# An inverse transform stage on 64-row instead of 128-row matmul tiles, with a new instruction order

## The chip, the cores and the metric

The kernel runs on one core of a Trainium2 chip. The metric is the device time of one launch in microseconds (us). A core has a matmul engine (TensorE, PE in the profile; its weight loads are listed apart as PEld), a vector engine (VectorE, DVE), a scalar engine (ScalarE, ACT), GpSimd (POOL) and a queue engine that issues most transfers (SyncE, SP). Each engine works through its own list of instructions in order and waits for the others by semaphores.

## What is computed

Two layers, each a long causal convolution with gates (A) and a feed-forward block (B), on 2048 positions of 512 channels. Both layers use the same k, v and filters, so the convolution result `y` is the same in both and the kernel computes it once.

```python
def _A_ref(q, k, v, shift_k, ssm_k, ssm_D):
    for t in range(ks):                      # ks = 4 taps
        k_shift = k_shift + k_pad[:, t:t + S, :] * shift_k[:, ks - 1 - t][None, None, :]
    kv = k_shift * v
    kv_f = rfft(kv padded to 2S, axis 1); kf_f = rfft(ssm_k padded to 2S)
    y = irfft(kv_f * kf_f)[:, :S, :]  (bfloat16)
    y = y + kv * ssm_D[None, None, :]
    return q * y

def _B_ref(x, w1, b1, w2, b2):
    y = _layernorm(x, axis=-1)
    h = _gelu(jnp.einsum("bsd,df->bsf", y, w1) + b1)
    return jnp.einsum("bsf,fd->bsd", h, w2) + b2

x = A_q
x = x + _A_ref(_layernorm(x, axis=-1), A_k, A_v, A_shift_k, A_ssm_k, A_ssm_D)
x = x + _B_ref(_layernorm(x, axis=-1), B_w1, B_b1, B_w2, B_b2)
# and the same two lines once more
```

## The kernel before

**Staging.** The 2048 positions are treated as two halves of 1024. For each half, the filter and the gated input go through a transform in two matmul stages. `stage1` makes eight tiles (names h1_0, h1_1 for the filter of the first and the second half, x1_0, x1_1 for the input). `stage2` makes eight more (h2_0, h2_1, x2_0, x2_1). The filter's spectrum is copied to a partner buffer by a DMA exchange (`swap`, eight transfers of 256 KB). VectorE multiplies the spectra (line 475, tag x2_0 for the first half). The inverse has two stages: `inverse1` (i1_0, i1_1; lines 677 to 704) and `inverse2` (i2_0, i2_1; line 706 on). Around that stand the transposes of the raw filter (`turn`, tags ht0 and ht1, line 561), the four-tap filter (fir0 to fir7), and thirteen blocks of the two layers: normalize and gate (q, y), normalize again (z), first feed-forward matmuls with gelu (m1, lines 920 and 925), second matmuls and add (m2, lines 954 and 958). Blocks 0 to 8 belong to the first half and fill the engines while the second half's transform runs.

**inverse1.** Each of its eight tiles (j = 0 to 7) takes eight channel groups, and for each group two products p and q, [128 x 128] each, against a 128-row table `R_U`. In i1_0 (`split` False) that is 16 matmuls a tile: a 128x128 weight load and 128 moving columns each. In i1_1 (`split` True) the upper and the lower 64 rows are separate matmuls: 32 matmuls a tile, each with a 64x128 weight load and 64 moving columns, which leaves out the half of the table that is zero for those rows; the two row halves write to two different PSUM banks. The output of a tile is the same [128 x 1024] in both; it is brought to SBUF by one instruction on ScalarE or VectorE (line 480 or 481, called an eviction here). `inverse2` multiplies over all eight tiles of i1, so it begins after the last of their evictions. Tiles j = 0 to 3 need the first 64-channel-group products (g = 0) of all eight x2_0 tiles, j = 4 to 7 the second (g = 1).

**Order.** Nothing is scheduled at run time. The program is a list of 1187 numbered operations. `SEQ` gives the order in which they are put on the engines' queues, `ENGS` names the engine (p, a, v for GpSimd, ScalarE, VectorE) of each operation that has a choice, and `BANKS` the first PSUM bank of each PSUM tile. All three are tables that were found by a search and written out. A tile of these stages takes two banks of 2 KB per partition, so there are four places (banks 0, 2, 4, 6); a matmul tile waits until the eviction of the tile that had its place before is done. `sync` derives all semaphore waits from data and banks.

**Numbers used below.** As each engine's list is in order, an operation's instruction is found by counting along its engine's part of `SEQ`:

| operations | what |
|---|---|
| 75/76, 77/78, ... 89/90 | h2_0 tiles 0 to 7: matmuls / eviction |
| 133/134, 129/130 | x1_0 tiles: matmuls / eviction |
| 139/140, 141/142, 145/146 | last three ht1 tiles: 8 transposes / eviction |
| 147/148, ... 161/162 | h1_1 tiles 0 to 7: matmuls / eviction |
| 163/164, 167/168, ... 191/192 | x2_0 tiles 0 to 7: matmuls / eviction; the two numbers after a pair are its products on VectorE (line 475) |
| 218/219, ... 232/233 | i1_0 tiles j = 0 to 7: matmuls (line 695) / eviction |
| 234 to 243 | i2_0, five tiles (line 717), matmuls / eviction |
| 244 to 267 | h2_1: matmuls and two combinations each (line 788) |
| 284 to 287 | four loads of v for the second half (SP) |
| 268 to 275 | the second half's exchange (SP) |
| 396 | first gate product of block 0 (y0), needs the first i2_0 tile |
| 404 | first transposes of block 0 (line 908) |

In the profile's order, ScalarE's nineteen evictions from 30.37 us on are 176, 164, 88, 188, 168, 150, 180, 192, 184, 160, 162, 142, 158, 156, 221, 225, 223, 231, 233; the next three are 227, 152, 235.

Of the kernel before, what the change touches and what calls it, by code (L numbers as in the profile page):

```python
# [36 lines left out]
class Prog:  # L37
# [361 lines left out]
def bass_interleave_layers__ssm_conv_h3__mixer_channel_mlp__prompt_kernel(  # L399
# [38 lines left out]
    R_1, R_2, R_3, R_8, R_4, R_5, R_6 = [place(n) for n in (8192, 8192, 8192, 11776, 8192, 8192, 8192)]  # L438
# [334 lines left out]
    P.op(POOL, lambda e: e.tensor_copy(SG, sg), 190.0, reads=[sg], writes=[SG])  # L773

    P.tag = "i1_0"
    inverse1(R_1, R_2, R_3, False)
    P.tag = "i2_0"
    inverse2(R_3, R_YT[0])

# [215 lines left out]
```

## Time and profile before

| | us |
|---|---|
| median of 3 runs (lowest, highest) | 236.24 (235.94, 237.43) |
| the profiled execution, whole | 235.91 |
| its span, first to last instruction | 234.0 |
| PE busy | 222.7 |
| DVE busy | 178.7 |
| ACT busy | 164.5 |
| POOL busy | 55.5 |

The granted TensorE clock is 1.00 throughout. The difference between 235.91 and 234.0 (1.9 us) lies around the span. Times in the views are us from the span's start. In a row of the order of time, the first number is the start, the second the duration, `x` the count of merged instructions, and in brackets stands the idle time before it and what ended it. A busy matmul row includes the pipeline's latency, so a single 128-column matmul shows 219 ns while eight tiles of sixteen take 7.38 us together.

### The profile page before, as it was taken

To read this page: it belongs to the slowest core of one execution; us is meant where nothing else is said; L and a number is where in the kernel's file an instruction comes from. 1 tells how busy PE (TensorE), PEld (TensorE's weight loads), DVE (VectorE), ACT (ScalarE), POOL (GpSimd) and SP (SyncE) were. 2 spreads that over 40 slices of the span, in tenths; PEclk is the share of its full clock that TensorE was granted. 3 is DMA by queue.
4 is the path that set the end of the run, shared out by engine and by line. 5 is a ranking of instruction groups with operands and counts; after the bars stand their busy time and mean duration, and the time that the engine had idled before them with its cause. 6 is when DMAs were issued, how large, how long until landed. Compare 5 with 4: busy or idle time off the path is not lost.

```text
span 234.0 us, 6498 instructions
## 1 busy us (share of the span) xinstructions
PE 222.7 (95%) x2743; PEld 147.1 (63%) x2765; DVE 178.7 (76%) x362; ACT 164.5 (70%) x262; POOL 55.5 (24%) x113
## 2 busy tenths in 40 slices
PE   7989887999999999999999999999999999999995
PEld 3878776967868596677966576644444444444454
DVE  0699998999999999999999988781777569410222
ACT  2789999989968688999879986488058216802710
POOL 2270132006403405639303331204011120200000
PEclk9999999999999999999999999999999999999999
DMA  6999489928994360033500313401300130170202
GB/s 185 381 386 305 147 229 274 324 65 150 144 211 126 70 158 3 1 48 72 155 4 3 90 24 68 134 3 22 69 0 3 28 62 0 23 115 0 90 0 92
DMA packets 40106, 24.93 MB, mean 107 GB/s; under 512 B 23591, under 2 KB 33677, under 8 KB 40077
## 3 DMA queue, kind: packets, MB, share of 16 engines
q1 hardware_dynamic: 39778, 24.36, 39.7%
q8 instruction: 22, 0.36, 0.7%
q10 hardware_dynamic: 298, 0.16, 0.4%
q14 instruction: 8, 0.06, 0.1%
HBM read 13.23 MB, written 2.10 MB: 66 GB/s over the span
## 4 chain that ended last, share of the span: by engine, by line
PE 58%; DVE 24%; ACT 10%; issue 2%; POOL 2%; DMA 2%; SPq 0%; DVEq 0%
PE ps L920 23%; PE ps L954 23%; DVE ar L475 13%; ACT ar L480 9%; PE ps L695 4%; DVE sm L831 3%; PE ps L590 2%; DMA ar<-in_A_ssm_k_dram 2%; DVE ar L672 2%; DVE ar L958 2%; DVE ar L641 2%; PE ps L717 1%; POOL sm L836 1%; PE ps L578 1%; PE ps L635 1%
## 5 line engine op out<-in xcount | busy, mean ns | idle before, releaser
L925 ACT ACTIVATE ar<-ps,sm 128x256 bf16<-128x256 f32 (+5 forms) x143 | 65.7, 523 | 33.2 <-PE ps L920 32.9
L920 PE MATMUL ps<-ar 128*128 128x256 bf16 (+5 forms) x569 | 81.9, 297 | 0.4 <-ACT ar L480 0.2
L480 ACT ACTIVATE ar<-ps 128x1024 bf16<-128x1024 f32 (+3 forms) x77 | 71.1, 998 | 11.0 <-PE ps L578 3.4
L954 PE MATMUL ps<-ar 128*128 128x512 bf16 (+1 forms) x323 | 75.9, 379 | 1.5 <-issue 0.6
L920 PEld LDWEIGHTS ps<-ar 128*128 128x128 bf16 (+1 forms) x572 | 52.9, 100 | 27.5 <-ACT ar L480 1.1
L475 DVE TENSOR_TENSOR ar<-ar 128x512 bf16<-128x512 bf16 (+2 forms) x104 | 62.7, 646 | 1.5 <-ACT ar L480 0.8
L954 PEld LDWEIGHTS ps<-ar 128*128 128x128 bf16 (+1 forms) x341 | 32.4, 98 | 35.3 <-ACT ar L925 0.4
L958 DVE TENSOR_TENSOR ar<-ar,ps 128x512 bf16<-128x512 bf16 x31 | 20.8, 680 | 32.9 <-PE ps L954 32.9
L831 DVE BATCH_NORM_STATS2 sm<-ar 128x6 f32<-128x512 bf16 x64 | 42.5, 685 | 0.5
L856 ACT ACTIVATE ar<-ar,sm 128x512 bf16<-128x512 bf16 x39 | 30.6, 813 | 12.9 <-DVE sm L843 8.8
L836 POOL TENSOR_SCALAR sm<-sm 128x2 f32<-128x2 f32 (+2 forms) x22 | 9.9, 449 | 89.0 <-DVE sm L832 88.8
L838 POOL TENSOR_TENSOR sm<-sm 128x2 f32<-128x2 f32 (+2 forms) x26 | 21.7, 834 | 25.1 <-DVE sm L836 23.1
L590 PE MATMUL ps<-ar 128*128 128x64 bf16 x512 | 18.4, 193 | 1.5 <-DVE ar L481 0.7
L578 PE MATMUL ps<-ar 128*64 128x128 bf16 x512 | 17.9, 221 | 1.8 <-ACT ar L480 1.2
L590 PEld LDWEIGHTS ps<-ar 128*128 128x128 bf16 x512 | 16.8, 98 | 3.6 <-DVE ar L481 1.3
L578 PEld LDWEIGHTS ps<-ar 128*64 128x64 bf16 x512 | 14.9, 110 | 4.8 <-ACT ar L480 1.9
L481 DVE CAST ar<-ps 128x1024 bf16<-128x1024 f32 x12 | 14.6, 1218 | 1.2 <-PE ps L578 0.9
L846 POOL TENSOR_SCALAR sm<-sm 128x1 f32<-128x1 f32 x34 | 15.1, 460 | 1.6
L695 PE MATMUL ps<-ar 64*128 64x64 bf16 (+1 forms) x384 | 12.4, 203 | 1.0 <-DVE ar L475 0.9
L695 PEld LDWEIGHTS ps<-ar 64*128 64x128 bf16 (+1 forms) x384 | 11.8, 113 | 2.2 <-DVE ar L475 1.0
L857 DVE TENSOR_SCALAR ar<-ar,sm 128x512 bf16<-128x512 bf16 x25 | 10.3, 415 | 2.7 <-POOL sm L846 2.5
L788 DVE SCALAR_TENSOR_TENSOR ar<-ar,sm,ps 128x512 bf16<-128x512 bf16 x16 | 11.1, 740 | 0.3 <-PE ps L590 0.3
(45 smaller groups left out, 93.5 us busy)
## 6 DMA issues: line engine op xcount, KB each, us to landing
ar<-ar SPq DMA_DIRECT2D x16, 256.0 KB, 4.0
ar<-tab_s SPq DMA_DIRECT2D x9, 256.0 KB, 6.3
ar<-in_A_ssm_k_dram SPq DMA_DIRECT2D x8, 256.0 KB, 5.9
ar<-in_A_q_dram SPq DMA_DIRECT2D x8, 256.0 KB, 4.4
ar<-in_A_v_dram SPq DMA_DIRECT2D x8, 256.0 KB, 5.0
out_dram<-ar SPq DMA_DIRECT2D x7, 256.0 KB, 2.5
ar<-in_B_w_dram SPq DMA_DIRECT2D x4, 344.0 KB, 5.2
ar<-in_B_w_dram SPq DMA_DIRECT2D x5, 256.0 KB, 5.2
```

Source lines behind the costliest of these rows:

```text
L475: return P.op(eng, lambda e: e.tensor_tensor(o, a, b, op), dur, reads=[a, b] + list(more), writes=[o])
L480: return e.activation(dst, src(), AF.Copy)
L578: r = e.matmul(Q(tl, 64 * ri, 64, i * 128, [1, 128]), w, m, start=True, stop=True)
L590: r = e.matmul(Q(tl, 0, 128, i // 8 * 512 + i % 8 * 4, [32, 16], [1, 4]), w, m, start=True, stop=True)
L695: r = e.matmul(Q(tl, 0, 128, i, *([32, 16], [1, 4]) if split else ([1, 128],)), w, m, start=n == 0, stop=n == 1)
L831: P.op(DVE, lambda e, sj=sj, x=x: e.bn_stats(sj, x), 600.0, reads=[x], writes=[sj])
L838: P.op(POOL, lambda e: e.tensor_tensor(r, v, hf, ALU.pow), 420.0 + 149.0 * n, reads=[v, hf], writes=[r])
L856: return e.activation(o, x, AF.Identity, bias=u, scale=r)
L920: r = e.matmul(Q(tl, 0, rows, 0, [1, w]), a, m, start=dk == 0, stop=dk == 3)
L925: P.op(ACT, lambda e, dst=dst, tl=tl, rows=rows, bias=bias, w=w: e.activation(dst, Q(tl, 0, rows, 0, [1, w]), AF.Gelu_apprx_tanh, bias=bia ...
L954: r = e.matmul(Q(tl, 0, 128, 0, [1, 512]), ins[fc][0], ins[fc][1], start=fc == 0, stop=fc == 10)
L958: P.op(DVE, lambda e, x=x, tl=tl: e.tensor_tensor(x, x, Q(tl, 0, 128, 0, [1, 512]), ALU.add), 604.0, reads=[x], writes=[x], tile=tl)
```

## The change

The first half's call takes the form of the second half's, and the three tables are replaced. The number of operations stays 1187, the lengths of the tables as well. No new function is called.

```diff
@@ (from line 773 on)
     P.tag = "i1_0"
-    inverse1(R_1, R_2, R_3, False)
+    inverse1(R_1, R_2, R_3, True)
     P.tag = "i2_0"
     inverse2(R_3, R_YT[0])
```

```diff
     SEQ = (
...
-        84, 145, 88, 187, 165, 171, 188, 96, 177, 167, 95, 172, 168, 149, 97, 296, 150, 146, 179, 98, 183, 170, 180,
-        195, 191, 173, 210, 157, 192, 208, 174, 202, 169, 184, 201, 159, 189, 196, 161, 303, 160, 207, 181, 155, 211,
-        185, 162, 203, 141, 193, 206, 142, 194, 224, 166, 158, 220, 190, 156, 186, 218, 178, 436, 221, 222, 182, 225,
+        84, 145, 88, 187, 188, 165, 96, 171, 177, 167, 95, 168, 149, 172, 97, 150, 98, 296, 179, 146, 195, 170, 180,
+        191, 210, 173, 196, 159, 192, 208, 174, 183, 201, 169, 184, 157, 207, 161, 189, 303, 211, 160, 155, 193, 203,
+        202, 181, 162, 185, 194, 141, 166, 142, 224, 190, 158, 220, 186, 178, 156, 218, 182, 436, 221, 582, 222, 219,
...
     ENGS = (
-            "pvavvvvvavpvpapapaaavaaaaavaavaavavvvppvvvaavvaaavaavvaaaaaaaaavvaaaaavaaaavaaaaaaapppvaaaaaaaaaaaaaaaaaa"
+            "pvavvvvvavpvpapapaaavaaaaaaaavaavavvvvpvvvaavvaaavaavvaaaaaaaaavvaaaavaaaavaaaaaaavpppaaaaaaaaaaaaaaaaaa"
...
     BANKS = (
-            "26624320240260660466027405640260464422140204626240406006442460424046462022442640460444626002206020640220"
+            "26624320240260660466027405640260464422140204626024406006442462424046462002442240460640446202220006040402"
...
```

The entries of the tables in and just before the changed stage that differ:

| operation | before | after |
|---|---|---|
| 78 (eviction, h2_0 tile 1) | VectorE | ScalarE, between 122 and 134 |
| 176 (eviction, x2_0 tile 3) | ScalarE | VectorE, between 90 and 584 |
| h1_1 tile of 157/158 | bank 2 | bank 0 |
| h1_1 tile of 159/160 | bank 4 | bank 2 |
| h1_1 tile of 161/162 | bank 0 | bank 4 |
| i1_0 tile of 218/219 | bank 2 | bank 0 |
| i1_0 tile of 224/225 | bank 0 | bank 2 |
| order of h1_1 matmuls | 157, 159, 161, 155 | 159, 157, 161, 155 |

The ht1 tile of 141/142 stays on bank 4; the tile that has bank 4 just before it is 159/160 before and 161/162 after. ScalarE's order from 88 to 235 is the same in both (88, 188, 168, 150, 180, 192, 184, 160, 162, 142, 158, 156, 221, 225, 223, 231, 233, 227, 152, 235), and so is TensorE's order of the i1_0 tiles (224, 220, 218, 222, 230, 232, 228, 226).

Later in the order: one i2_1 eviction goes from ScalarE to VectorE; of the small statistics operations up to the last product sum of the second half (tag sum), four go from GpSimd to VectorE and one back; the number of TensorE operations ahead of the first i1_1 tile is 204 in both. On SP, the v loads 286 and 287 stood ahead of all exchange transfers of the second half, and now stand behind the first (268) and the second (271) of them. Normalizations of the q and z steps change engine in both directions (ten from ScalarE to VectorE, twelve the other way).

More of the change, by code (lines that the diff above doesn't have):

```diff
@@ L45 @@
         0, 46, 8, 45, 35, 2, 6, 3, 5, 36, 12, 9, 1, 10, 11, 25, 4, 44, 217, 7, 56, 197, 15, 50, 16, 57, 14, 13, 47,
[3 rows of a table removed]
[3 rows of a table added]
         111, 68, 394, 117, 33, 112, 395, 119, 29, 123, 118, 124, 143, 32, 144, 131, 120, 81, 113, 474, 213, 79, 82,
[50 rows of a table removed]
[50 rows of a table added]
     ENGS = (
-            "pvavvvvvavpvpapapaaavaaaaavaavaavavvvppvvvaavvaaavaavvaaaaaaaaavaaaaavaaaavaaaaaaapppvaaaaaaaaaaaaaaaaaa"
-            "avaaaaaaaaapvapvvavpvppaappvvpvaavpaappaappaappaappaappavppvappaappaappvappaapvaapvavvavvvvvapvvvvvppvaa"
-            "avvvvaappavvapvavavpvvava")
+            "pvavvvvvavpvpapapaaavaaaaaaaavaavavvvvpvvvaavvaaavaavvaaaaaaaaavvaaaavaaaavaaaaaaavpppaaaaaaaaaaaaaaaaaa"
+            "avaaaaaaavapvapvvavpvvpaappvvppaavpaappaappaappaapvaappavppvavvaappaappvappaappaavpvaavvvvaaappaavvppaav"
+            "vvvvavvvpaavavvvavvvvavav")
     BANKS = (
-            "26624320240260660466027405640260464422140204626240406006442460424046462022442640460444626002206020640220"
-            "04023022660051677767117660640311026376367637332542537030213654742352762454741476061377362300423726574027"
-            "07315704314621527766215047034261015330227471565340011503350731745320154030276054756")
+            "26624320240260660466027405640260464422140204626024406006440462424046462002442240460640446202220006040402"
+            "20201200661071175760610706761354673263266337232241657763022741351603667540723566150777263632670156541304"
+            "32172437425406650215234545702175254221347040501613506136707146104347507513610560112")
     def __init__(self, nc):
```

100 rows, old and new, of the table SEQ are left out of this document.

## The prediction

> **What bounds the kernel now.** I read the page's head first, then busy time by stretch, then the chain that ended last, then the order of time around the changed stage.
>
> ```profile
> span 234.0 us, 6498 instructions
> PE 222.7 (95%) x2743; PEld 147.1 (63%) x2765; DVE 178.7 (76%) x362; ACT 164.5 (70%) x262; POOL 55.5 (24%) x113
> ```
>
> ```profile
> 41.00:56.00 15.00, 14.08 (x241) 11.76 (x243) 14.61 (x33) 13.79 (x17) 1.91 (x5) 1.00 0.67 176
> 56.00:121.00 65.00, 63.92 (x925) 48.29 (x931) 64.11 (x109) 57.26 (x114) 25.57 (x41) 1.00 0.45 97
> 145.00:234.00 89.00, 86.24 (x436) 42.66 (x441) 46.00 (x111) 40.08 (x69) 9.48 (x20) 1.00 0.19 44
> ```
>
> After the stretch and its length come the busy times of PE, PEld, DVE, ACT and POOL. PE's 95% suggests that any matmul time saved is saved in full. The stretches say otherwise: up to 121 us DVE is as full as PE (64.11 of 65.00), and only after 145 us is PE alone full.
>
> ```profile
> 41.32 7.39 PE ps L695 x128
> 48.73 6.59 ACT ar L480 x8
> 108.48 12.51 DVE ar L475 x11
> 124.17 1.67 PE ps L954 x7
> ```
>
> The chain passes through the changed stage (128 matmuls, 41.32 to 48.71), leaves it by an eviction on ACT at 48.73, is carried by DVE until the products and sums of the second half end (108.48 + 12.51 = 120.99), and then by PE. The first i1_1 tile starts at 121.44 (row below), and the same 204 PE operations stand ahead of it in both orders, so what PE has left from there is the same work. The question is thus how far 121.44 moves.
>
> **The tile itself.**
>
> ```profile
> 41.31 7.22 PEld L695 LDWEIGHTS ps<-ar 128*128 128x128 bf16 x128 [1.04 <-DVE ar L475]
> 121.44 1.68 PEld L695 LDWEIGHTS ps<-ar 64*128 64x128 bf16 x96 [0.43 <-ACT ar L925]
> 121.44 2.57 PE L695 MATMUL ps<-ar 64*128 64x64 bf16 x128
> 125.77 1.68 PEld L695 LDWEIGHTS ps<-ar 64*128 64x128 bf16 x96 [0.42 <-issue]
> ```
>
> A 128-row tile takes 7.39 / 8 = 0.92 us. Of the 64-row form, three tiles back to back take 1.68 (0.56 each), and four with one wait for a place 2.57 (0.64 each). The change removes 128 matmuls with their loads and adds 256 small ones: 8 x (0.92 - 0.64) = 2.2 to 8 x (0.92 - 0.56) = 2.9 us less PE. Entering the 64-row form costs between nothing and the 0.42 us of idle time that the last row has with nothing to wait for; I take none, as the tile has a wait to hide it in. [...]
>
> **What else sets the stage: places and evictions.**
>
> ```profile
> 25.46 4.74 ACT L480 ACTIVATE ar<-ps 128x1024 bf16<-128x1024 f32 x5 [0.25 <-PE ps L590]
> 30.37 17.65 ACT L480 ACTIVATE ar<-ps 128x1024 bf16<-128x1024 f32 x19 [0.17 <-PE ps L590]
> 48.73 6.59 ACT L480 ACTIVATE ar<-ps 128x1024 bf16<-128x1024 f32 x8 [0.71 <-PE ps L695]
> ```
>
> ```profile
> 27.22 1.23 DVE L481 CAST ar<-ps 128x1024 bf16<-128x1024 f32 x1 [0.33 <-PE ps L590]
> 28.96 0.67 DVE L481 COPY ar<-ps 128x1024 bf16<-128x1024 bf16 x1
> 29.65 1.23 DVE L481 CAST ar<-ps 128x1024 bf16<-128x1024 f32 x1
> 31.39 1.21 DVE L481 CAST ar<-ps 128x1024 bf16<-128x1024 f32 x1
> 36.35 1.29 DVE L475 TENSOR_TENSOR ar<-ar 128x1024 bf16<-128x1024 bf16 x2 [0.82 <-ACT ar L480]
> ```
>
> ```profile
> 28.50 0.99 PEld L590 LDWEIGHTS ps<-ar 128*128 128x128 bf16 x32 [0.24 <-DVE ar L481]
> 31.45 0.52 PEld L590 LDWEIGHTS ps<-ar 128*128 128x128 bf16 x16 [0.30 <-ACT ar L480]
> 39.70 0.57 PEld L561 LDWEIGHTS ps<-ar 128*128 128x128 bf16 x8 [0.44 <-ACT ar L480]
> 55.37 0.23 PEld L908 LDWEIGHTS ps<-ar 128*128 128x128 bf16 x4 [0.40 <-ACT ar L480]
> ```
>
> From 30.37 to 48.02 ACT runs nineteen evictions without a gap, one each (17.65 - 1.03) / 18 = 0.92 us (a single one spans 1.03: the last of the nineteen starts at 46.98 and ends at 48.02). The twentieth is that of the last i1_0 tile (48.73, after 0.71 of waiting for PE). [...] In the new order ACT loses more than this ahead of the stage, at three places.
>
> 1. Op 78 comes to ACT. ACT's third of the five evictions is 78 at 27.3 instead of 134; 134 moves from 27.3 to 28.2 (ends 29.2), 130 from 28.2 to 29.1. The second of the two matmul tiles at 28.50 (89) needs 134's place: 28.95 becomes 29.3, and its eviction on DVE (90) starts at 30.0 for 29.65.
> 2. Op 176 goes to DVE behind 90. It was ACT's at 30.37; on DVE it starts at 30.0 + 1.13 = 31.1 (starts 29.65 and 31.39 stand 1.74 apart with one 0.6 us operation between, so 1.13 an eviction) and ends at 32.35. The tile 87 at 31.45 waited for exactly this place; it now starts at 32.4 and its loads end at 32.9. Its eviction 88 starts some 0.15 later (28.50 + 0.99 = 29.49 to 29.65 in the rows for 89 and 90). It is ACT's third of nineteen: 32.2 becomes 33.05, **0.85 later**. ACT has the same operations from there, back to back, so all of them come 0.85 later. On DVE the next eviction (84, 31.39) moves to 31.1 + 1.13 + 0.6 = 32.9. From 31.39 to the idle time ahead of 36.35 it has 36.35 - 0.82 - 31.39 = 4.1 us of work, so the product that waited there comes at 32.9 + 4.1 = 37.0: the idle time absorbs most of the move, 0.6 stays.
> 3. The transposes 141 (39.70, released by ACT's 160) have bank 4. Before, 160 freed it and ACT had 162 to do meanwhile; now 162 itself frees it. 162 starts at 33.05 + 8 x 0.92 = 40.4 and ends at 41.45; the transposes take 0.57 of loads; ACT's next operation is their eviction 142, at about 41.5 + 0.57 + 0.15 = 42.2 where it stood at 40.5. So ACT idles 0.75 us. From both sides: no less than the 0.57 that the loads take, no more than 0.9. The like pattern at 55.37 (four transposes between two ACT operations) takes 0.49, from the eviction's end at 48.73 + 6.59 = 55.32 to ACT's next start at 55.81 (below), with 0.23 of loads.
>
> ```profile
> 55.81 0.60 ACT L480 ACTIVATE ar<-ps 128x512 bf16<-128x512 bf16 x1 [0.49 <-PE ps L908]
> 40.57 4.30 DVE L475 TENSOR_TENSOR ar<-ar 128x1024 bf16<-128x1024 bf16 x7
> 45.39 1.22 DVE L481 CAST ar<-ps 128x1024 bf16<-128x1024 f32 x1
> 49.81 0.11 PEld L717 LDWEIGHTS ps<-ar 128*128 128x128 bf16 x2 [0.26 <-ACT ar L480]
> 51.19 0.88 DVE L475 TENSOR_TENSOR ar<-ar 128x512 bf16<-128x512 bf16 x2
> ```
>
> Then 158, 156 and the first i1_0 eviction 221: 42.2 + 3 x 0.92 = 45.0 instead of 43.3. Six i1_0 evictions are ACT's, so the last (227) starts at 45.0 + 5 x 0.92 = 49.6, if its tile is ready. The tiles in between wait for places: 220 for 142's eviction, 218 and 222 for 158 and 156; 232 for 219's on DVE (45.39 + 1.22, and 0.6 later with DVE's products, which ended at 44.87: 47.2); 226 for 231's (fourth, 45.0 + 2.76 + 1.03 = 48.8), and with 0.56 it ends at 49.4. So 227 starts at 49.6 for 48.73: **0.9 us later**, its tile only just ready. The 2.2 to 2.9 us that PE saves here become waits for places. i2_0 starts at 50.7 for 49.81, and the first gate product of block 0, at 51.19 behind it, at 52.1.
>
> **From 52 us to 121 us.** DVE and PE are both full there, so the 0.9 travels on, less the waits that it fills.
>
> ```profile
> 66.24 1.40 DVE L788 SCALAR_TENSOR_TENSOR ar<-ar,sm,ps 128x512 bf16<-128x512 bf16 x2 [0.28 <-PE ps L590]
> 98.34 0.69 DVE L958 TENSOR_TENSOR ar<-ar,ps 128x512 bf16<-128x512 bf16 x1 [0.52 <-PE ps L954]
> L843 DVE SCALAR_TENSOR_TENSOR sm<-sm 128x4 f32<-128x4 f32 x6 | 1.0, 161 | 4.5 <-POOL sm L838 4.5
> ```
>
> DVE's idle time is 65.00 - 64.11 = 0.89, most of it these two waits for PE (0.28 + 0.52). DVE also gets three small operations net from POOL, 0.16 each by the last row at most: 0 to 0.5, I take 0.2 since they overlap their neighbours. DVE would thus end its sums at 121.0 + 0.9 + 0.2 - 0.8 = 121.3 with both waits gone and 122.1 with none. PE has 55.37 + 0.9 = 56.3 for the first transposes of block 0 and the same work up to i1_1 (121.44 - 55.37 = 66.1): 122.3, or 121.3 if its 1.08 of idle time in the stretch went. Between 121.3 and 122.3 I take the middle nearer the upper end of PE's, as PE's waits there are short ones by ACT: 122.0, **0.55 later**. Costed at nothing: the normalizations that change engine and the i2_1 eviction given to DVE, all behind 121 us, where DVE is busy 46.0 and ACT 40.1 of the last 89 us; if that cover were gone, 1.2 us each at most. The sum: 235.91 + 0.55 = 236.5 against the profiled execution's own time, which stands 0.33 below the median of the runs. I name 236.5 for the new median too: the median of three holds one run at 237.43, so the two differ by less than my sum is sure.
>
> **Rivals.** About 1% is what a measurement of this kernel can tell from no change.
>
> *PE's saving falls through whole.* For it: PE 95%, 63.92 of 65.00. Against it: the last eviction is bound by ACT, DVE is full too, and PE has the same work behind i1_1. Time: 235.91 - 2.4 = 233.5. Chance 0.07.
>
> *The hold-ups ahead of the stage don't bite* (1 to 3 hidden in gaps that I didn't see), and 227 moves up by the 0.71 that ACT waited. DVE's ends by its idle time limit it: 0.39 in 41 to 56 and part of the 0.89. Time: 235.91 - 0.9 = 235.0. Chance 0.2.
>
> *The 64-row tiles are no shorter here than 0.92.* Then 226 ends at 48.8 + 0.92 = 49.7 and 227 starts at 49.8: 236.6, nearly my time. Chance 0.06.
>
> *Slower: the late loads of v.*
>
> ```profile
> 58.18 0.47 SPq L460 DMA_DIRECT2D ar<-in_A_v_dram  x1
> 73.23 0.60 DVE ar L672
> ar<-in_A_v_dram SPq DMA_DIRECT2D x8, 256.0 KB, 5.0
> ```
>
> SP issued the last v load (287) at 58.18. It now stands behind two exchange transfers that need the h2_1 tiles 0 to 3; their last combination is the twelfth of sixteen on DVE, and the thirteenth starts at 66.24 in the row above, so they end by 66.2 + 0.9 = 67.1 at the latest. Two exchanges and two loads take some 2.4 us of issuing (0.47 for the load in the row, taken as 0.6 each), and 5.0 to land: 74.5. The first product that reads v stood at 73.23 and by its new place on DVE comes near 76. From a landing of 6.5 us on, every further microsecond falls on DVE, which is full: at 8.5 us, 236.5 + 2 = 238.5. Chance 0.1.
>
> My forecast (235.9 to 237.2 by its own bounds) has 0.5; the rest, 0.07, is what I don't see.
>
> **How the numbers follow.** 234.7 to 237.7 holds the forecast, the unshortened tile and the second rival, and part of the slower one's lower end: 0.8. Faster by over 1% (below 233.9): the first rival, with a little of the second, 0.08. Slower by over 1% (above 238.6): half the last rival and half the unseen, 0.09. Within 1%: 0.83.
>
> **What would show it.** Right: ACT idle ahead of op 142 near 42 us, released by the line-561 transposes; i1_0 tiles of 0.56 with waits between; i2_0 starting near 50.7; the first i1_1 matmul near 122.0. The second rival: i2_0 before 49.5 and i1_1 before 121. The late loads: a wait of VectorE's line 672 for a DMA near 76. Wrong altogether: if ACT's nineteen evictions still run without a gap, or PE waits more than before behind 121 us.

## The result, and the profile after

| | before | after |
|---|---|---|
| median of 4 runs each, us | 236.09 | 240.49 |
| lowest, highest, us | 235.87, 237.43 | 238.96, 241.13 |
| profiled execution, us | 235.91 | 238.96 |
| its mean granted clock | 1.00 | 1.00 |

The ratio after / before is 1.0169, with an interval from 1.0139 to 1.0200. The change makes the kernel slower, by 4.4 us in the medians, where 236.5 (234.7 to 237.7) was forecast. The profiled execution of after is its fastest; the other three took 239.94, 241.04 and 241.13 with a mean granted clock of 0.993. So there are two things to explain: 3.05 us that the trace shows at full clock, and about 1.5 us more that it doesn't show.

The head of the page of after:

```profile
span 237.2 us, 6773 instructions
PE 224.0 (94%) x2893; PEld 144.9 (61%) x2893; DVE 180.6 (76%) x366; ACT 165.8 (70%) x263; POOL 57.7 (24%) x114
```

Span and instructions say little by themselves; the order of time says where the time came from. First ScalarE in the trace of after (start, duration, count, idle time before and its releaser), from op 88 on:

```profile
33.40 2.01 ACT L480 ACTIVATE ar<-ps 128x1024 bf16<-128x1024 f32 x2 [0.68 <-PE ps L590]
35.59 6.67 ACT L480 ACTIVATE ar<-ps 128x1024 bf16<-128x1024 f32 x7 [0.18 <-PE ps L590]
43.06 11.27 ACT L480 ACTIVATE ar<-ps 128x1024 bf16<-128x1024 bf16 x13 [0.81 <-PE ps L561]
```

The first row starts with 88, the second ends with 162 (its seventh, at 41.22), and the third starts with 142 and holds 227 as its ninth (at 50.49). The uninterrupted run of nineteen evictions is gone: ACT idles 0.81 ahead of 142, for the transposes of line 561.

TensorE's weight loads in the trace of after show the same stage from the other side:

```profile
42.30 0.58 PEld L561 LDWEIGHTS ps<-ar 128*128 128x128 bf16 x8 [1.35 <-ACT ar L480]
42.95 0.62 PEld L695 LDWEIGHTS ps<-ar 64*128 64x128 bf16 x32
44.13 0.61 PEld L695 LDWEIGHTS ps<-ar 64*128 64x128 bf16 x32 [0.56 <-ACT ar L480]
45.05 0.61 PEld L695 LDWEIGHTS ps<-ar 64*128 64x128 bf16 x32 [0.30 <-ACT ar L480]
45.97 0.61 PEld L695 LDWEIGHTS ps<-ar 64*128 64x128 bf16 x32 [0.31 <-ACT ar L480]
46.88 1.39 PEld L695 LDWEIGHTS ps<-ar 64*128 64x128 bf16 x68 [0.31 <-ACT ar L480]
49.27 1.08 PEld L695 LDWEIGHTS ps<-ar 64*128 64x128 bf16 x60 [0.99 <-issue]
51.59 0.13 PEld L717 LDWEIGHTS ps<-ar 128*128 128x128 bf16 x2 [0.28 <-DVE ar L857]
```

A tile is 32 loads in some 0.6 us. The second to the fifth of the eight tiles each wait for an eviction on ACT. One gap is of another kind: 68 loads, then 0.99 us of nothing, then 60 more. 68 is two tiles and four loads, so TensorE stopped inside a tile, where it waits for no engine ("issue"). i2_0 starts at 51.59 (before: 49.81).

Three later places, in DVE's and PE's order of time in after:

```profile
66.32 2.08 DVE L788 SCALAR_TENSOR_TENSOR ar<-ar,sm,ps 128x512 bf16<-128x512 bf16 x3 [0.37 <-PE ps L590]
105.10 0.16 DVE L843 SCALAR_TENSOR_TENSOR sm<-sm 128x2 f32<-128x2 f32 x1 [0.60 <-POOL sm L838]
```

```profile
123.52 2.56 PE L695 MATMUL ps<-ar 64*128 64x64 bf16 x128
148.21 0.61 PE L920 MATMUL ps<-ar 128*128 128x256 bf16 x4 [0.57 <-ACT ar L925]
172.78 7.51 PE L920 MATMUL ps<-ar 128*128 128x512 bf16 x34 [0.15 <-DMA ar<-ar]
```

i1_1 starts at 123.52 (before: 121.44). Behind it, PE waits for a gelu on ACT at 148.21, and at 172.78 for a transfer. In the trace of before the same matmuls (by count at 145.74 and 173.76) stand inside rows without a wait:

```profile
144.75 3.00 PE L920 MATMUL ps<-ar 128*128 128x256 bf16 x26
169.65 9.66 PE L920 MATMUL ps<-ar 128*128 128x512 bf16 x43
```

Counted by place in TensorE's order, after is 2.08 us later than before at i1_1, 2.81 behind the first of these waits and 3.14 behind the second. The chain that ended last in after passes through the second of these waits: it comes by SP's queue and a transposing DMA of block 10.

```profile
165.86 0.88 SPq L900
169.40 3.33 DMA ar<-ar
172.78 9.67 PE ps L920 x44
```

Start of the same operation, after minus before, all in the two profiled executions:

| operation | before | after | difference |
|---|---|---|---|
| 68, ACT's last h1_0 eviction | 17.33 | 17.65 | +0.32 |
| 88, eviction of h2_0 tile 6 | 32.20 | 33.40 | +1.20 |
| 162, eviction | 39.48 | 41.22 | +1.74 |
| 142, eviction of the transposes | 40.45 | 43.06 | +2.61 |
| 227, last i1_0 eviction | 48.73 | 50.49 | +1.76 |
| 234, i2_0 | 49.81 | 51.59 | +1.78 |
| 360, i1_1 | 121.44 | 123.52 | +2.08 |
| last addition on VectorE | 231.70 | 234.85 | +3.15 |

Over half of the loss at full clock is there when i2_0 starts. The 0.32 at 17 us is older than anything that the prediction looked at, but it is no measure of the order: in a second trace of the kernel before (below, "before once more") op 68 starts at 17.86, later than in after.

```profile
17.86 1.02 ACT L476 ACTIVATE ar<-ps 128x1024 bf16<-128x1024 f32 x1 [0.46 <-PE ps L574]
```

Over the traces below, op 68 starts at 17.23 to 18.15 with before's head and at 17.29 to 18.03 with after's (the kernel with a longer warm-up left out), and from 68 to 88 it takes 14.85 to 15.11 with the one and 15.74 to 15.89 with the other (where 78 and 176 stand as in after). So the order costs 0.88 there (15.75 - 14.87 in the pair of the table). In before a late start of the head is mostly taken up by the time that ACT waits ahead of 227: in before once more this is 0.41 instead of 0.71, and i2_0 starts at 49.95, only 0.14 later. After has no such wait.

### The profile page after: what moved, and what is told of

Same layout as the page of the kernel before. It is cut to its first block, busy times and chain, and to the rows that moved or that the text cites. A ratio compares the mean times of both kernels' runs of the same rounds, so it can differ in the third digit from the quotient of the medians.

```text
span 237.2 us, 6773 instructions
## 1 busy us (share of the span) xinstructions
PE 224.0 (94%) x2893; PEld 144.9 (61%) x2893; DVE 180.6 (76%) x366; ACT 165.8 (70%) x263; POOL 57.7 (24%) x114
## 4 chain that ended last, share of the span: by engine, by line
PE 55%; ACT 17%; DVE 16%; DMA 5%; SPq 2%; POOL 2%; issue 1%; DVEq 0%; ACTq 0%
PE ps L920 22%; PE ps L954 21%; ACT ar L480 12%; DVE ar L475 6%; PE ps L590 4%; ACT ar L925 4%; DVE sm L831 4%; DMA ar<-ar 3%; DMA ar<-in_A_ssm_k_dram 2%; PE ps L578 2%; DVE ar L481 2%; SPq L900 2%; PE ps L695 2%; DVE ar L641 1%; PE ps L717 1%; ACT ar L856 1%
## 5 line engine op out<-in xcount | busy, mean ns | idle before, releaser
L954 PE MATMUL ps<-ar 128*128 128x512 bf16 (+1 forms) x341 | 79.0, 379 | 0.0
L856 ACT ACTIVATE ar<-ar,sm 128x512 bf16<-128x512 bf16 x41 | 31.7, 808 | 12.4 <-DVE sm L843 9.3
L590 PE MATMUL ps<-ar 128*128 128x64 bf16 x512 | 19.3, 193 | 3.0 <-ACT ar L480 1.4
L836 POOL TENSOR_SCALAR sm<-sm 128x2 f32<-128x2 f32 (+2 forms) x16 | 4.4, 277 | 65.3 <-DVE sm L832 65.1
L481 DVE CAST ar<-ps 128x1024 bf16<-128x1024 f32 x13 | 15.8, 1218 | 1.4 <-PE ps L590 0.8
L846 POOL TENSOR_SCALAR sm<-sm 128x1 f32<-128x1 f32 x42 | 16.2, 403 | 1.8
L695 PE MATMUL ps<-ar 64*128 64x64 bf16 x512 | 10.6, 195 | 2.0 <-ACT ar L480 1.0
L695 PEld LDWEIGHTS ps<-ar 64*128 64x128 bf16 x512 | 9.5, 114 | 3.5 <-ACT ar L480 1.6
L857 DVE TENSOR_SCALAR ar<-ar,sm 128x512 bf16<-128x512 bf16 x23 | 9.0, 402 | 3.4 <-POOL sm L846 2.5
L481 DVE COPY ar<-ps 128x1024 bf16<-128x1024 bf16 (+1 forms) x8 | 5.0, 624 | 8.6 <-PE ps L561 7.7
```

The lines of the kernel that those rows point to most:

```text
L481: return e.tensor_copy(dst, src())
L590: r = e.matmul(Q(tl, 0, 128, i // 8 * 512 + i % 8 * 4, [32, 16], [1, 4]), w, m, start=True, stop=True)
L695: r = e.matmul(Q(tl, 0, 128, i, *([32, 16], [1, 4]) if split else ([1, 128],)), w, m, start=n == 0, stop=n == 1)
L856: return e.activation(o, x, AF.Identity, bias=u, scale=r)
L954: r = e.matmul(Q(tl, 0, 128, 0, [1, 512]), ins[fc][0], ins[fc][1], start=fc == 0, stop=fc == 10)
```

## The experiments

Main theory after the trace: the new order delays the stage and the tail, and the smaller tiles gain nothing since ACT's evictions bind. First rival: the 64-row form itself costs, by the stop inside a tile or by something in the executions at 0.993. A form and an order can be tried apart. Times are medians in us; each ratio is against runs of the kernel before on the same chip. Tables of order, engines and banks are shown here by the rule that makes them.

**The form alone, the order alone, and nothing.**

```diff
-    inverse1(R_1, R_2, R_3, False)
+    inverse1(R_1, R_2, R_3, True)
```

> Tables of before, with i1_0 alone in the 64-row form. Order theory (the time is lost to the new order, not to the form): in the old order the places come free early, the last i1_0 tile is ready at 47.7 us and its eviction on ACT starts at 47.9 instead of 48.73, so i2_0 starts 0.7 to 0.85 us earlier (near 49.0) and the kernel takes 235.0 to 236.1 us. Form theory (the 64-row tiles themselves cost, by mode changes or by their two-bank output): i2_0 starts at 50.5 or later and the kernel takes 237.5 us or more.

```diff
-SEQ, ENGS, BANKS = before
+SEQ, ENGS, BANKS = after
     inverse1(R_1, R_2, R_3, False)
```

> Tables of after, with i1_0 in the 128-row form. Order theory: still about as slow as after, 239 to 242 us; the last i1_0 tile starts near 49.7 and now takes 0.92 for 0.56, so i2_0 starts 0.2 to 0.5 us later than the 51.6 of after. Form theory: back to 236 to 237 us.

The kernel before, unchanged, once more:

> The kernel before, unchanged, for the granted clock of each execution. If the clock falls because TensorE idles in the 64-row stage, this kernel, whose 128-row stage keeps TensorE busy, shows 1.00 in all or nearly all executions, 235.4 to 236.9 us. If half-clock windows are a chance event of any kernel, 0.993 shows here too in about as many executions as with the 64-row form (8 of 10).

Measured: the form alone 238.26 (235.58 to 239.00, ten runs), ratio 1.0060 [1.0021, 1.0098]; the order alone 239.29, ratio 1.0127 [1.0107, 1.0147]; before once more 236.39, ratio 1.0015 [0.9999, 1.0030]. So the order alone carries about 2.9 us, at a clock of 1.00 in four of four executions. The form alone is slower too and misses the 235.0 to 236.1 expected by the order theory, but with a wide spread that goes with the clock: two executions at 1.00 took 235.58 and 235.94, as expected, and eight at 0.993 or 0.986 took 236.95 to 239.00. The trace of the form alone fell into the latter. Its weight loads, in order of time:

```profile
46.13 1.16 PEld L691 LDWEIGHTS ps<-ar 64*128 64x128 bf16 x64 [1.31 <-DVE ar L471]
47.86 0.14 PEld L691 LDWEIGHTS ps<-ar 64*128 64x128 bf16 x3 [0.57 <-DVE ar L477]
49.21 1.56 PEld L691 LDWEIGHTS ps<-ar 64*128 64x128 bf16 x61 [1.21 <-issue]
```

And by stretch (busy time of PE, PEld, DVE, ACT and POOL, then the granted clock, the DMA share and GB/s):

```profile
42.64:46.05 3.41, 2.29 (x128) 2.17 (x126) 3.41 (x7) 3.41 (x5) 0.00 (x0) 1.00 1.02 369
46.05:49.46 3.41, 1.76 (x81) 1.55 (x83) 3.08 (x7) 2.79 (x3) 0.00 (x0) 1.00 0.39 136
49.46:52.87 3.41, 3.32 (x91) 3.11 (x85) 1.59 (x3) 1.90 (x2) 0.00 (x0) 0.50 0.02 5
```

The reader sees two things. TensorE stops for 1.21 us three loads into a tile, with nothing to wait for. And from 49.46 to 52.87 the granted clock is 0.50: a full stage at half speed, with DVE and ACT half idle behind it. One such stretch takes 0.5 x 3.41 / 236.8 = 0.7% off the mean clock, which would account for the 0.993 of after's three slower executions; 0.986 would be two. Those executions have no trace, so where their stretch lay isn't shown. Op 234 starts at 52.70 here.

**Where the order costs.** Two kernels take their form from after and mix the orders: all operations ahead of h2_1 (op 244) in one order, the rest in the other. A third, with 128-row tiles, takes before's order up to i1_1 (op 360) and after's behind it. Two more undo one place each in the kernel with after's order and 128-row tiles.

```diff
-SEQ = SEQ_after
+head = set(SEQ_after[:SEQ_after.index(244)])
+SEQ = [i for i in SEQ_before if i in head] + [i for i in SEQ_after if i not in head]
```

> 64-row form; what stands ahead of the first h2_1 tile in the order of after is put in before's order, with before's engines and banks; the rest is after's. Order theory: i2_0 near 49.0 (2.5 us earlier than after's 51.6), of which nearly all reaches the start of i1_1 (121.3 to 121.8 for 123.5); the tail's two waits stay, so 236.5 to 239 us. If the head is not the cause, 239.5 us or more.

```diff
-SEQ = SEQ_before
+head = set(SEQ_before[:SEQ_before.index(244)])
+SEQ = [i for i in SEQ_after if i in head] + [i for i in SEQ_before if i not in head]
```

> 64-row form; what stands ahead of the first h2_1 tile in the order of before is put in after's order, with after's engines and banks; the rest is before's. Order theory: i2_0 near 51.6, and the time is before's plus 1.3 to 1.9 us for the head alone, 237.3 to 238.1 us. If the head's delay is absorbed behind it, 236.0 to 236.8 us, and the loss lies in the rest of the order.

Measured: old head 239.65 (237.91 to 240.81), ratio 1.0140 [1.0081, 1.0200], clocks 0.993, 0.993, 1.00 and 0.986; new head 237.74 (237.42 to 238.66), ratio 1.0069 [1.0042, 1.0095], clock 1.00 in three of four. The new head comes out as expected (237.3 to 238.1; its i2_0 at 51.56), the old head misses its 236.5 to 239. Neither part alone carries the loss. As medians the old head looks worse, which would clear the head; but its one execution at full clock took 237.91, and its trace has the same stop inside a tile and a stretch of 3.41 us at half clock:

```profile
44.93:48.34 3.41, 1.55 (x69) 1.34 (x71) 3.27 (x7) 3.27 (x4) 0.00 (x0) 1.00 0.20 77
48.34:51.75 3.41, 3.41 (x93) 3.31 (x93) 1.54 (x2) 1.58 (x2) 0.00 (x0) 0.50 0.02 5
```

With 64-row tiles the orders couldn't be compared cleanly, so the three that follow have 128-row tiles, and all their executions have a clock of 0.999 or 1.00.

```diff
-ENGS[78], ENGS[176] = "a", "v"
+ENGS[78], ENGS[176] = "v", "a"
-        478, 90, 215, 163, 205, 479, 83, 164, 176, 480, 584, 87,
+        478, 90, 215, 163, 205, 479, 83, 176, 164, 480, 584, 87,
```

> Tables of after, 128-row form (its time without this edit: 239.3 us, i2_0 at 52.0), with the evictions 78 and 176 back on their engines of before. Order theory, places 1 and 2 of the prediction: eviction 88 comes back by 0.7 to 1.0 us (33.5 to about 32.6), ACT's row of evictions and i2_0 with it (51.0 to 51.4), and the kernel takes 238.2 to 238.8 us. If the gap of ACT ahead of eviction 142 or TensorE's own tiles set i2_0 alone, it stays at 51.7 or later and the time within 0.3 us of 239.3.

```diff
-BANK[157], BANK[159], BANK[161], BANK[218], BANK[224] = 0, 2, 4, 0, 2
+BANK[157], BANK[159], BANK[161], BANK[218], BANK[224] = 2, 4, 0, 2, 0
-        191, 210, 173, 196, 159, 192, 208, 174, 183, 201, 169, 184, 157, 207, 161, 189,
+        183, 191, 210, 173, 196, 157, 192, 208, 174, 201, 169, 184, 159, 207, 161, 189,
```

> Tables of after, 128-row form, with the banks of the three h1_1 and two i1_0 tiles and the order of the matmuls 157, 159, 183 and 191 of before. Order theory, place 3 of the prediction: the transposes 141 no longer wait for eviction 162, ACT's 0.9 us gap ahead of eviction 142 goes, i2_0 starts 0.6 to 0.9 us earlier (51.1 to 51.4) and the kernel takes 238.4 to 238.8 us. If it does not count, i2_0 stays at 51.7 or later.

```diff
-SEQ, ENGS, BANKS = before
+head = set(SEQ_before[:SEQ_before.index(360)])
+SEQ = SEQ_before[:SEQ_before.index(360)] + [i for i in SEQ_after if i not in head]
```

> 128-row form; what stands ahead of the first i1_1 tile in the order of after is put in before's order, with its engines and banks; the rest is after's. If the tail of the new order costs by itself (TensorE's waits of 0.83 and 0.53 us in the profile of after, at 148 and 173 us), i1_1 starts at 121.3 to 121.7 and the kernel takes 0.8 to 1.3 us more than before. If those waits only follow from the late start, it takes the time of before within 0.3 us.

| kernel | 68 | 88 | 142 | i2_0 | i1_1 | median | ratio |
|---|---|---|---|---|---|---|---|
| after's order, 128 rows | 17.78 | 33.53 | 43.19 | 51.97 | 123.83 | 239.29 | 1.0127 [1.0107, 1.0147] |
| 78 and 176 back | 18.03 | 32.91 | 42.23 | 51.32 | 123.19 | 238.68 | 1.0097 [1.0080, 1.0113] |
| banks back | 17.35 | 33.10 | 41.70 | 50.80 | 122.67 | 238.73 | 1.0103 [1.0088, 1.0118] |
| after's tail alone | 17.46 | 32.32 | 40.59 | 49.71 | 121.35 | 236.77 | 1.0017 [1.0005, 1.0030] |

Both places are real. The starts in a row come from one execution, and they differ at 68 already, ahead of what the two edits touch; so they are best counted from 68. With 78 and 176 back, 88 follows 68 by 14.88 instead of 15.75, 0.87 less, and the median falls by 0.6. With the old banks ACT's idle time ahead of 142 is gone: its order of time, first with the evictions back, then with the banks back, reads

```profile
31.09 10.34 ACT L476 ACTIVATE ar<-ps 128x1024 bf16<-128x1024 f32 x11 [0.17 <-PE ps L586]
42.23 7.44 ACT L476 ACTIVATE ar<-ps 128x1024 bf16<-128x1024 bf16 x8 [0.80 <-PE ps L557]
```

```profile
37.11 12.03 ACT L476 ACTIVATE ar<-ps 128x1024 bf16<-128x1024 f32 x13
49.73 4.75 ACT L476 ACTIVATE ar<-ps 128x1024 bf16<-128x1024 f32 x6 [0.58 <-PE ps L691]
```

The 0.80 stays in the one and is missing in the other. i2_0 comes 1.17 earlier with the banks back, more than the 0.6 to 0.9 expected; but 0.43 of this is there at 68 already. Counted from 68, i2_0 starts at 34.19 in after's order with 128 rows and at 32.25 with before's order up to i1_1; of this 1.94, the two evictions take back 0.90 and the banks 0.74. The medians fall by 0.61 and 0.56. The tail costs some 0.4 us by itself (1.0017 x 236.29 - 236.29), less than the 0.8 to 1.3 that its two waits had let me expect. In its trace the wait for the gelu is still there, while the second one is not:

```profile
146.05 0.61 PE L916 MATMUL ps<-ar 128*128 128x256 bf16 x4 [0.57 <-ACT ar L921]
170.31 5.99 PE L916 MATMUL ps<-ar 128*128 128x512 bf16 x27
```

**The stop inside a tile, and the half clock.** The page of after lists the transfers that bring instructions (packets, MB, share of 16 engines):

```profile
q8 instruction: 23, 0.38, 0.7%
```

23 transfers stand beside PE's 2893 matmuls and 2893 loads. From these counts, an estimate: about 252 of PE's instructions for each, if this queue serves TensorE alone, which no view shows. A 64-row tile is 64 instructions (32 loads and 32 matmuls) in 0.56 us, so by this estimate four tiles use up a transfer in some 2.3 us; of the 128-row tiles with 32 instructions in 0.92 us it takes eight and 7.4 us. In the trace of after, one such transfer starts at 46.79 and ends at 47.67; TensorE's last load ahead of the stop ends at 48.27 (46.88 + 1.39), and the rest of the tile starts at 49.27, 1.6 us after the transfer's end. From 41 to 46 us the DMA engines were full in the form alone:

```profile
41.00:46.00 5.00, 2.67 (x133) 2.41 (x130) 5.00 (x10) 5.00 (x7) 0.31 (x1) 1.00 0.98 340
```

Theory: such a transfer (a refill) comes late behind the weight loads (`in_B_w` and others, issued by SP in this stretch), TensorE runs dry, and the low activity sets off the half clock. Rival: the stop belongs to the tile's place or mode, and no supply is involved. If it is supply, adding instructions ahead must move the stop to another matmul; and the loads, held back, must make it go away.

```diff
-        for i in range(7):
+        for i in range(3):
...
+        for i in range(68):
+            r = e.matmul(Q(tl, 0, 64, 0, [1, 128]), z[:, :64], z[:, :128], start=True, stop=True)
```

> Tables of before, 64-row form, and 64 small matmuls more in the warm-up (four of its large ones less), so that every later TensorE instruction stands 128 places further in the stream. Fetch theory (the 1.1 to 1.2 us gap after the third matmul of i1_0's seventh tile is a late refill of TensorE's instructions): the gap leaves this place and comes two tiles earlier, at or near the start of the fifth tile, where TensorE waits 1.2 us for products anyway; i2_0 then starts at 49.0 to 50.5 instead of 52.7. If the gap belongs to the tile (its form, its banks), it stays after the seventh tile's third matmul.

The change stands in the warm-up at the kernel's start: 64 more matmuls with their loads, 128 instructions, which is two 64-row tiles. Measured: 241.58 (240.57 to 242.44), ratio 1.0228 [1.0191, 1.0266]. The stop moved as the theory said, from the seventh tile to the fifth, again three loads in, with nothing to wait for:

```profile
48.36 0.15 PEld L693 LDWEIGHTS ps<-ar 64*128 64x128 bf16 x3 [0.85 <-DVE ar L471]
50.02 3.17 PEld L693 LDWEIGHTS ps<-ar 64*128 64x128 bf16 x125 [1.52 <-issue]
```

The expected start of i2_0 was missed: the longer warm-up made the whole head some 2.9 us later, so this run settles the place of the stop and no time (ACT's first eviction starts at 8.61; before: 5.70).

```diff
-            def f(e, ins=ins, tl=tl):
+            def f(e, ins=ins, tl=tl, fill=p == R_1):
+                for i in range(4 if fill else 0):
+                    g = i % 2
+                    r = e.matmul(Q(tl, 0, 128, 512 * g, [1, 512]), A(64 * g, 64, R_ID, [1, 128]), A(64 * g, 64, R_S2, [1, 512]), start=True, stop=True)
```

> Tables of before, 64-row form, and at the head of each i1_0 tile four matmuls of 512 columns more (two per row half), whose results are overwritten. Idle theory (the half-clock windows come when TensorE idles between the short tiles): about 0.43 us of busy time more a tile brings the stage back to the 128-row form's load, the clock is 1.00 in most executions, and the time is 235.8 to 237.0 us though more is computed. If the 64-row form as such brings the windows, 0.993 stays in most executions and the time is 238 us or more.

Here every 64-row tile of i1_0 has four extra matmuls of 512 columns, whose results the real ones overwrite, so that PE is busier and the tile takes 0.96 us. Measured: 238.60 (238.05 to 239.41), ratio 1.0108 [1.0070, 1.0145], clock 1.00 in four of four. The clock is as the idle theory expected, the time is not (235.8 to 237.0). The stop is still there, now in the sixth tile, after eleven of its own loads:

```profile
46.90 0.45 PEld L694 LDWEIGHTS ps<-ar 64*128 64x128 bf16 x11
48.92 0.44 PEld L694 LDWEIGHTS ps<-ar 64*128 64x128 bf16 x21 [1.57 <-issue]
```

Counted in TensorE's instructions from the start of i1_0 (eight more a tile), this is the same place: 5 x 72 + 8 + 22 = 390, against 6 x 64 + 6 = 390 in the form alone. And with the longer warm-up it is 4 x 64 + 6, 128 less.

So the stop and the half clock are two effects: here is the one without the other. In the kernel with the new head the half clock (44.38 to 47.79) even lies ahead of its stop:

```profile
44.38:47.79 3.41, 3.31 (x117) 2.94 (x112) 3.33 (x5) 3.41 (x5) 0.00 (x0) 0.50 0.76 250
```

```profile
49.24 1.08 PEld L691 LDWEIGHTS ps<-ar 64*128 64x128 bf16 x60 [0.79 <-issue]
```

The part of the theory by which the stop sets off the half clock by itself falls with this. It can add to the idle time: in the form alone it lies in the stretch of 3.41 us just ahead of the half clock.

```diff
     SEQ = (
-        195, 191, 173, 210, 157, 192, 208, 174, 202, 169, 184, 201, 159, 189, 196, 161, 303, 160, 207, 181, 155, 211,
+        195, 196, 191, 173, 157, 192, 174, 169, 184, 159, 189, 161, 303, 160, 181, 155,
...
+        222, 210, 208, 202, 201, 207, 211, 203, 206, 182, 225,
...
+        self.ops[210].preds[222] = "raw"
```

> Tables of before, 64-row form; eight loads of the feed-forward weights and biases, issued at 37 to 43 us, are held until i1_0's fourth tile, and the second load of i2_0's table moves ahead of them. If the instruction refill is late because these loads fill the DMA queues (98% busy from 41 to 46 us), the refill comes 1 to 2 us earlier than the 47.0 of the form alone and the gap after the seventh tile's third matmul goes or shrinks below 0.4 us; i2_0 near 49.5. If the refill only takes its own time, the gap stays near 1.1 us. The first m1 matmuls may wait for the held weights by up to 1 us.

This is the form alone, with eight loads of weights and biases held until the fourth i1_0 tile is done, and the second load of the i2_0 table moved ahead of them. Measured: **235.46** (235.12 to 237.28, ten runs), ratio 0.9979 [0.9958, 1.0000], clock 1.00 in ten of ten (before on the same chip: 235.91). The weight loads of the last four tiles of i1_0 in order of time, and the stretch from 41 us:

```profile
45.70 1.14 PEld L692 LDWEIGHTS ps<-ar 64*128 64x128 bf16 x64 [1.10 <-DVE ar L472]
47.42 1.14 PEld L692 LDWEIGHTS ps<-ar 64*128 64x128 bf16 x64 [0.58 <-DVE ar L478]
49.88 0.13 PEld L714 LDWEIGHTS ps<-ar 128*128 128x128 bf16 x2 [0.35 <-ACT ar L477]
```

```profile
41.00:46.00 5.00, 2.84 (x147) 2.59 (x148) 5.00 (x9) 5.00 (x7) 0.00 (x0) 1.00 0.09 24
```

DMA share 0.09 instead of 0.98, each tile runs whole, and i2_0 starts at 49.88 (49.5 was expected; before: 49.81). Against the form alone (1.0021 to 1.0098) the intervals are apart. That TensorE stops inside a tile behind these loads, and doesn't when they are held, is shown by this. That a late refill is the link between the two was the author's reading and isn't shown, nor what passes in the 1.6 us between the end of the transfer in after and TensorE's next instruction.

```diff
+222, 210, 208, 201, 207, 211, 203, 202,
...
+        self.ops[210].preds[222] = "raw"
```

> The kernel after, with the weight and bias loads held until i1_0's fourth tile and the second load of i2_0's table ahead of them. Fetch theory: the 0.99 us gap inside i1_0's seventh tile goes, and the granted clock is 1.00 in all or nearly all executions (after: 1 of 4); i2_0 starts 0.1 to 0.5 us earlier than 51.6, since ACT's evictions bind there; 238.3 to 239.2 us against the 240.5 of after. If the half-clock windows come from the 64-row form or from the waits for places, 0.993 stays in most executions and the time is 239.8 us or more.

The same in the kernel after, with seven loads held behind 222: 239.15 (238.87 to 239.79), ratio 1.0129 [1.0106, 1.0151], clock 1.00 in four of four. The stop inside the tile is gone, and every wait left in the stage is one for an engine:

```profile
46.66 1.86 PEld L692 LDWEIGHTS ps<-ar 64*128 64x128 bf16 x96 [0.30 <-ACT ar L477]
49.41 0.61 PEld L692 LDWEIGHTS ps<-ar 64*128 64x128 bf16 x32 [0.89 <-ACT ar L477]
51.28 0.13 PEld L714 LDWEIGHTS ps<-ar 128*128 128x128 bf16 x2 [0.29 <-DVE ar L854]
```

What is left is the loss of the order alone, 1.0127: with it, the 64-row form gains nothing.

**The account.** Of the 4.4 us in the medians, the order has 2.9 (order alone). The form in that order has the rest, 0.9 (by the ratios 1.0169 and 1.0129) to 1.3 (240.49 - 239.15), and it goes with the clock: at 1.00 after took 238.96, which lies inside the 238.87 to 239.79 with held loads. So the stop costs after nothing that shows at full clock, and the 0.993 of three executions is what the form adds (the order alone has 1.00 in four of four). That holding the loads removed it here isn't settled: four executions of each are few, and TensorE's longest lack of work in this order lies ahead of the stop and is the same in both (1.76 and 1.75 us busy of 3.41, table at the end). In before's order it is shown that holding them brings the clock back to 1.00, by ten executions of ten against two of ten. Of the order's 2.9, the two evictions have 0.6, the banks 0.6 and the tail 0.4 to 0.5, as medians. The remaining 1.2 to 1.3 wasn't split: what ACT loses between 88 and 162 beyond these edits, and what is lost between 52 and 121 us, are in it.

## Why the prediction was wrong

The mechanism of the stage was forecast rightly: places and ACT's evictions set its end, and the shorter tiles gain nothing. What failed is the step by which ACT's evictions from 88 on keep their pace, the step by which waits of DVE absorb part of the delay up to i1_1 (2.08 us later, for 0.55), and the tail, which was put at nothing (1.06 us). The clock had no term at all.

- **The 64-row tile** was sized right: 0.57 us back to back (64 loads in 1.14, with held loads), and its saving became waits for places, as forecast. Entering the form cost nothing that shows, as assumed: in after, its first load starts at 42.95, 0.07 behind the transposes' last (42.30 + 0.58). With held loads, in before's order, the shorter tiles bring i2_0 no earlier: it starts at 49.88 for 49.81, while ACT is busy for 5.00 of 5.00 us in the row shown above and PE for 2.84. DVE is as full there (5.00), and the waits shown are for its products and evictions.
- **Steps 1 and 2** were right in size: 88 was forecast 0.85 later and came 1.20 later, of which 0.32 is the head's start in this execution; counted from 68 it is 0.88. 90 (30.31) and the product behind the wait (37.30) stand by the same 0.3 later than forecast:

```profile
30.31 2.36 DVE L481 CAST ar<-ps 128x1024 bf16<-128x1024 f32 x2 [0.76 <-PE ps L590]
37.30 8.51 DVE L475 TENSOR_TENSOR ar<-ar 128x1024 bf16<-128x1024 bf16 x14
```

- **Step 3** was right in kind and nearly in size: from 162 to 142 it takes 1.84 instead of 0.97, so 0.87 more for a forecast 0.75. What failed is the step "ACT has the same operations from there, back to back": from 88 to 162 ACT lost another 0.54 (7.82 instead of 7.28, and the same 7.82 or 7.83 in three more traces of after's order), part of it the 0.18 of waiting for PE at 35.59. From 142 on ACT runs without a gap, as forecast (7.43 to the start of 227, for 7.4).
- **The stage's delay** was thus 1.78 at i2_0 instead of 0.9: 0.54 from ACT's run, and 0.32 by which the head started later in this execution, make up the difference. The 0.32 lies within the spread of executions and isn't shown to be the order's.
- **52 to 121 us**: the step that lets DVE's two waits for PE absorb part of the delay failed. In the stretch of 65 us that ends just ahead of i1_1, DVE of after idles 1.06 instead of 0.89:

```profile
58.08:123.08 65.00, 64.70 (x924) 47.75 (x925) 63.94 (x110) 56.38 (x113) 21.66 (x37) 1.00 0.48 103
```

  The wait of 0.52 went, that of 0.28 became 0.37 (at 66.32), and a new one for GpSimd came at 105.10 (0.60). i1_1 came 2.08 later and not 0.55.
- **The tail** was costed at nothing. At full clock 1.06 us was lost there in the profiled execution, 0.73 and 0.33 at the two waits above; alone it costs 0.4. Taking idle shares as cover was the mistake: DVE and ACT are half idle there, but a gelu or a transfer that comes late still stops PE, which is full.
- **The clock and the stop inside a tile** had no term in the sum. The trace of before shows neither: its granted clock is 1.00, and its 128 loads of i1_0 stand in one row without a gap. The executions at 0.993 have 0.9 to 1.3 us of the result; the stop cost after nothing that shows at full clock.
- **The rivals**: the slower one, the late loads of v, did not bite. SP issues them from 69.10 on, and the first product that reads v has no wait ahead of it:

```profile
69.10 0.62 SPq L460 DMA_DIRECT2D ar<-in_A_v_dram  x1
76.91 1.26 DVE L672 TENSOR_TENSOR ar<-ps,ar 128x512 bf16<-128x512 f32 x2
```

  The saving that falls through whole is refuted by the stage's waits. That the hold-ups don't bite is refuted by i2_0 at 51.59. That the tiles are no shorter is refuted by the 0.57. The loss went by a way that none of the rivals named: several small delays of the new order that add up on a path with no slack, and the lower clock. One of the prediction's own signs of being wrong altogether did come: PE waits more behind 121 us.

## What to carry to other kernels

When an order is replaced as a whole, compare the two orders from the first operation to the last; a sum made around the edited stage misses what is lost behind it, and idle shares of other engines are no cover for an engine that is full. Before a difference between two traces is put down to a change, look at the same start in a second trace of the unchanged kernel: here 0.53 us lay between two of them at op 68. A faster form of a stage can be tried with the old order and its late-needed loads moved out of its way: that was the only version here that came out ahead (235.46, ratio 0.9979, with an interval that touches 1). If the granted clock differs between executions of one kernel, look for a stretch in which PE lacks work: the five kernels here with executions below 0.995 have 3.41 us in which PE was busy for 1.76 us or less (table below).

## What the runs showed of the hardware

**The stop inside a tile.** TensorE stopped for 0.79 to 1.57 us inside a tile, waiting for no engine, in all six kernels that ran 64-row tiles behind a full DMA stretch (a DMA share of 0.94 to 1.03 over 3.4 to 5 us). Its place moved with the count of instructions (390 into i1_0 in two kernels, 128 less with 128 more ahead), and it went away in both kernels with held loads (a share of 0.09 from 41 to 46 us with before's order, 0.26 from 40.60 to 44.01 us in after). That TensorE lacks instructions there is the reading that fits these runs; no view shows what it waits for. In after's time at full clock the stop is hidden (238.96, for 238.87 to 239.79 with held loads); in the kernel with the extra matmuls, also at full clock, the 1.57 us of its stop lie on the way to i2_0, which starts at 52.50 (before: 49.81).

**The half clock.** In four traces 3.41 us at a granted clock of 0.50 follow a stretch of the same length in which PE was busy for 1.55 to 1.79 us, some half of the time, with no single idle time over 1.6 us (the longest that a row shows is 1.52, with the longer warm-up). For each kernel, the lowest PE busy time in any 3.41 us between 36 and 53.4 us (steps of 0.2 us, the profiled execution), beside the executions with a clock below 0.995:

| kernel | lowest PE busy, us of 3.41 | executions below 0.995 |
|---|---|---|
| before once more | 2.26 | 0 of 10 |
| order alone | 1.99 | 0 of 4 |
| held loads | 1.94 | 0 of 10 |
| extra matmuls | 1.83 | 0 of 4 |
| after | 1.76 | 3 of 4 |
| after, held loads | 1.75 | 0 of 4 |
| new head | 1.75 | 1 of 4 |
| form alone | 1.51 | 8 of 10 |
| old head | 1.50 | 3 of 4 |
| longer warm-up | 1.07 | 4 of 4 |

The other three with 128-row tiles stand at 1.99 to 2.32, with none of 18. The row of that view for the form alone, then the stretch just ahead of the half clock in the kernel with the new head:

```profile
45.00:48.41 3.41, 1.51 (x67) 1.30 (x67) 3.41 (x7) 3.41 (x5) 0.00 (x0) 1.00 0.70 252
```

```profile
40.97:44.38 3.41, 1.79 (x64) 1.62 (x66) 3.15 (x6) 2.60 (x4) 1.37 (x2) 1.00 0.94 297
```

At 1.83 us and above none of 46 executions has a clock below 0.995, at 1.51 and below 15 of 18 have, and at 1.75 and 1.76 it is 4 of 12. (The 13 executions of before that the form alone was measured against are not in the table; one of them took 238.08 at 0.993, without a trace here.) In the four traces with a half-clock stretch it starts at 49.46 (form alone), 48.34 (old head), 44.38 (new head) and near 49.35 (longer warm-up: 0.99 from 46.00 to 49.41, 0.51 from 49.40 to 52.81), and in the 3.41 us just ahead PE was busy for 1.76, 1.55, 1.79 and some 1.7 us (with the longer warm-up 1.87 from 45.80 on and 1.67 from 46.00 on). The traces of after and of after with held loads have 1.76 and 1.75 us, at a mean clock of 1.00. So in these runs the half clock goes with PE's lack of work. What decides at 1.75 and 1.76, and why executions of one kernel differ, isn't shown, and the executions without a trace can't show where their half-clock stretch lay.
